# Second-layer weights decoded at other steps, and four places instead of five for the second product, in an attention and two feed-forward layers kernel

## The chip, the cores and the metric

One core of a Trainium2 chip. The metric is the device time of one execution in microseconds. All matrix work runs on TensorE, elementwise work on VectorE and ScalarE; transfers are issued by SyncE (SP) and ScalarE.

## The reference, cut to what matters

```python
def reference(q, k, v, moe_w_in, moe_w_out, moe2_w_in, moe2_w_out):
    # windowed attention: B 4, heads 8, S 576, D 64, window of 64 positions
    scores = q @ k.transpose(0, 1, 3, 2) / sqrt(64)          # masked outside the window
    attn = softmax(scores)
    x = (attn @ v).transpose(0, 2, 1, 3).reshape(2304, 512)
    # first layer, d_ff 2048
    h = x @ moe_w_in
    x = (maximum(h, 0) + log1p(exp(-abs(h)))) @ moe_w_out    # softplus
    # second layer, d_ff 2048
    h = x @ moe2_w_in
    g = where(h >= 1, h, where(h <= -1, 0, (h + 1) ** 2 / 4))
    return g @ moe2_w_out
```

All of it is float32.

## The kernel before

Precision. A float32 product is made of three matmuls of high and low parts (`high`, `low`): high by high, high by low, low by high.

First layer. The 2304 tokens are worked in blocks of 512, 256, 512, 512 and 512 (blocks 0 to 4). A block takes 16 steps, one for each tile f of 128 columns of d_ff (the small block takes two tiles in a step). A step has `g1` (L391, twelve matmuls into a bank h), `softplus` on ScalarE twice (L414 gh, L415 e), the low part on VectorE (L416 gl), and two steps later (LAG) `g2` (L402, twelve matmuls into four banks y). While block i is multiplied, the attention of block i+1 is made in four chunks of 128 tokens, put between the steps as items: score products (L273), copies of the scores (L297 on ScalarE, L301 on VectorE, L295 where a chunk begins a sequence), maximum (L305, L306), eight exponentials (L310) on ScalarE, normalising (L317) into p, transposes of p (L327) on TensorE, masking into pt (L337), products with v (L354), and the two parts of x (L359, L362). Block 4 has no attention beside it. The opening is ordered by a list written by hand (START); after it a scheduler orders each engine's instructions by when they can run.

Weights. w_in and w_out of a tile f lie side by side as 64-bit words, 512 KB of raw words for a half (one of the two matrices' tiles). `load_w` (L145, on SP) brings a half into `raw`, a ring of four buffers shared with o, xs and wf. `begin_half` (L162, ScalarE) and `end_half` (L167, L168, L169, VectorE) turn it into float32 in a bits buffer, of which there are two; these two are also the buffers of c in the second layer. The second layer's 32 halves are decoded in blocks 2 and 3, one at every step of the program (`decode_w`), w_in and w_out in turn (the scheduler brings the first of them forward into block 1), and each is stored to DRAM (wd, L204, 256 KB) at the next step. Later the w_in halves come back in pairs as ab (`load_pair`, L453), and the w_out halves in pairs as wf (`load_wout`, L473), to be split into wh (L178) and wl (L185) in block 4 and in the first two pairs of the second layer.

Second layer. 2304 tokens in three blocks of 768, and in each block eight pairs of tiles f: 24 pairs. x2, the first layer's result, is read back (xs, L493) and cut into pieces (`term` L500, `split_x` L505, L506). A pair is one step of a fast matrix product with seven products (`product`, L535, six matmuls of 384 columns each); `combine` (L459 to L468) makes the seven pieces of w_in. `total` adds (L526) or copies (L524) a bank into c, with m1, u2 and m5 as kept banks; `quadratic` (L513 to L518) is the activation. The second product of the pair before, `second` (L550, six groups of six matmuls of 512 columns), is put between the products by `behind(0)` to `behind(5)`. In the last pair of a block the banks are copied (L553) and stored (L555).

## Time and profile before

| | us |
|---|---|
| three runs | 888.42, 886.96, 892.16 (median 888.42) |
| profiled execution | 889.04 |
| its span, first to last instruction | 887.3 |
| TensorE busy | 848.9 (96%) |
| VectorE busy | 578.4 (65%) |
| ScalarE busy | 409.2 (46%) |

The mean granted clock is 0.998 of full speed. TensorE is named PE in the views, VectorE DVE, ScalarE ACT, SyncE SP. The copies of a finished block into o (L425) begin at 156.4 us for block 0, 217.7 for block 1, 319.8 for block 2, 424.3 for block 3 and 512.9 for block 4; the second layer takes the rest. A name like `a<-ident,p` is what an instruction writes and reads; a name in brackets is what ended the idle time ahead of an instruction.

### The profile page before, as it was taken

Reading aid. Unit: us, or ns where it says so; the run is one execution under the profiler, and the core shown is the slowest. Engines: PE = TensorE matmul, PEld = TensorE weight load, DVE = VectorE, ACT = ScalarE, POOL = GpSimd, SP = SyncE. Lnnn points to the kernel's source line nnn. Section 1 sums busy time; section 2 is a strip of 40 time slices with the busy share of each in tenths; the row PEclk is TensorE's granted clock in tenths of the full one; section 3 lists DMA queues with packets and bytes.
Section 4 is the critical chain, followed back from the end, with each engine's and each line's share of the span. In section 5 each row is a group of like instructions: output and inputs, shape, how many; then the busy total and the mean of one; then the engine's idle time right before and its main releaser. Section 6 shows DMA issues by size and latency. Waiting matters only on the chain.

```text
span 887.3 us, 13141 instructions
## 1 busy us (share of the span) xinstructions
PE 848.9 (96%) x5032; PEld 716.3 (81%) x5032; DVE 578.4 (65%) x1101; ACT 409.2 (46%) x987; POOL 1.5 (0%) x10
## 2 busy tenths in 40 slices
PE   3799999999998999899999999999999999999998
PEld 2686666799877887688888898999898989988896
DVE  5998953764677256635344498667787768776653
ACT  4655622443434344433344474445655446454442
POOL 0000000000000000000000000000000000000000
PEclk9999999999999999999999999999999999999999
DMA  8677512843874157501412041010330101201001
GB/s 299 206 241 233 181 59 80 271 150 119 304 260 155 54 183 249 198 1 48 160 36 89 24 167 48 25 48 24 105 109 24 48 24 47 96 24 49 24 1 71
DMA packets 55118, 100.59 MB, mean 113 GB/s; under 512 B 5904, under 2 KB 25360, under 8 KB 55056
## 3 DMA queue, kind: packets, MB, share of 16 engines
q1 hardware_dynamic: 52672, 95.31, 32.7%
q10 hardware_dynamic: 2384, 4.46, 1.3%
q8 instruction: 39, 0.64, 0.3%
q14 instruction: 23, 0.19, 0.1%
HBM read 81.92 MB, written 17.83 MB: 112 GB/s over the span
## 4 chain that ended last, share of the span: by engine, by line
PE 76%; DMA 10%; DVE 8%; ACT 3%; issue 2%; SPq 1%; ACTq 0%; DVEq 0%
PE h L535 20%; PE y L402 15%; PE y L550 15%; PE h L391 15%; PE a L550 7%; DMA raw<-in_w 6%; DMA wd<-bits 3%; DVE pt L337 2%; DVE bits L168 2%; PE a L354 2%; ACT p L310 1%; DVE bits L169 1%; ACT bits L162 1%; PE a L273 1%; DVE bits L167 1%
## 5 line engine op out<-in xcount | busy, mean ns | idle before, releaser
L391 PE MATMUL h<-xh,area 128*128 128x512 f32 (+1 forms) x672 | 202.6, 371 | 1.7 <-ACT g L409 1.7
L535 PE MATMUL h<-area,ah 128*128 128x384 f32 x672 | 171.3, 335 | 0.0
L391 PEld LDWEIGHTS h<-xh,area 128*128 128x128 f32 x672 | 122.1, 190 | 24.5 <-issue 2.7
L535 PEld LDWEIGHTS h<-area,ah 128*128 128x128 f32 x672 | 123.3, 188 | 10.3
L391 PE MATMUL h<-xl,area 128*128 128x512 f32 (+1 forms) x336 | 121.7, 362 | 0.0
L535 PE MATMUL h<-area,al 128*128 128x384 f32 x336 | 112.5, 335 | 0.0
L514 ACT ACTIVATE e<-e 128x384 f32<-128x384 f32 x96 | 50.2, 524 | 95.9 <-DVE e L513 95.7
L402 PE MATMUL y<-gl,wh 128*128 128x512 f32 (+1 forms) x256 | 93.1, 363 | 0.0
L402 PE MATMUL y<-gh,wh 128*128 128x512 f32 (+1 forms) x256 | 92.9, 363 | 0.0
L402 PE MATMUL y<-gh,wl 128*128 128x512 f32 (+1 forms) x256 | 92.8, 363 | 0.0
L416 DVE TENSOR_TENSOR gl<-e,gh 128x512 fp32r<-128x512 f32 x56 | 38.6, 689 | 65.6 <-ACT e L415 65.6
L550 PE MATMUL y<-wh,gl 128*128 128x512 f32 x192 | 76.2, 397 | 0.0
L550 PE MATMUL y<-wl,gh 128*128 128x512 f32 x192 | 75.8, 395 | 0.0
L550 PE MATMUL y<-wh,gh 128*128 128x512 f32 x192 | 74.6, 389 | 0.0
L391 PEld LDWEIGHTS h<-xl,area 128*128 128x128 f32 x336 | 64.0, 191 | 9.4 <-issue 0.7
L414 ACT ACTIVATE gh<-h 128x512 fp32r<-128x512 f32 x56 | 33.2, 593 | 81.2 <-PE h L391 81.2
L518 DVE TENSOR_TENSOR gl<-e,gh 128x384 fp32r<-128x384 f32 x96 | 53.3, 555 | 18.1 <-ACT gh L517 17.9
L535 PEld LDWEIGHTS h<-area,al 128*128 128x128 f32 x336 | 63.0, 188 | 0.0
L517 ACT CAST gh<-e 128x384 fp32r<-128x384 f32 x96 | 49.3, 514 | 28.8 <-DVE e L515 28.7
L515 DVE TENSOR_TENSOR e<-c,e 128x384 f32<-128x384 f32 x96 | 53.2, 555 | 13.7 <-ACT e L514 12.3
L162 ACT ACTIVATE bits<-raw 128x512 f32<-128x512 f32 x48 | 32.0, 670 | 64.7 <-DMA wd<-bits 30.9
L310 ACT ACTIVATE p<-p,mx 128x64 f32<-128x64 f32 x144 | 48.1, 338 | 23.5 <-DVE mx L306 23.3
(104 smaller groups left out, 1347.5 us busy)
## 6 DMA issues: line engine op xcount, KB each, us to landing
raw<-in_w SPq DMA_DIRECT2D x64, 512.0 KB, 5.3
ab<-wd SPq DMA_DIRECT2D x24, 512.0 KB, 3.3
qt<-in_q SPq DMA_DIRECT2D x34, 256.0 KB, 4.7
vt<-in_v SPq DMA_DIRECT2D x32, 256.0 KB, 3.2
wd<-bits SPq DMA_DIRECT2D x32, 256.0 KB, 3.4
kt<-in_k SPq DMA_DIRECT2D x29, 256.0 KB, 4.7
xs<-x2d SPq DMA_DIRECT2D x12, 384.0 KB, 4.0
wf<-wd SPq DMA_DIRECT2D x8, 512.0 KB, 4.6
```

The costliest lines, as they stand in the source:

```text
L162: A.activation(t.bitcast(F32), raws[j][:, :, 1].bitcast(F32), AF.Copy, scale=2.0 ** -112)
L310: A.activation(k["sel"][:, i, :], k["sel"][:, i, :], AF.Softplus, bias=k["mx"][:, i:i + 1], scale=SCALE, accum_out=k["sm"][:, i:i + 1])
L391: T.matmul(h, w, x, start=i == 0, stop=i == len(ops) - 1)
L402: T.matmul(y[m][:, c0:c0 + n], w, x, start=begin and i == 0, stop=f == NF - 1 and i == len(ops) - 1)
L414: A.activation(gh, h, AF.Softplus)
L416: V.tensor_tensor(gl, e, gh.bitcast(F32), op=ALU.subtract)
L514: A.activation(e, e, AF.Square, bias=0.5, scale=0.5)
L515: V.tensor_tensor(e, c, e, op=ALU.max)
L517: A.copy(gh, e)
L518: V.tensor_tensor(gl, e, gh.bitcast(F32), op=ALU.subtract)
L535: T.matmul(bank, l[:, c], r[:, kc], start=begin and kc == i == 0, stop=kc == 1 and i == 2, skip_group_check=True)
L550: T.matmul(yw[t], l, r, start=p == j == i == 0, stop=p == NQ - 1 and j == 1 and i == 2)
```

## The change

1. Blocks 2 and 3 decode only w_in halves, one at every second step (`decode_win`), and store 16 halves to DRAM instead of 32. `load_w` for the second layer is issued after the store and not after the decode.
2. The w_out halves are decoded where they are split (`split_wout`): one at each step of block 4 from the fifth on (twelve), and one in each of the first four pairs of the second layer. They don't go through DRAM; wf and its eight loads of 512 KB are gone. The number of raw loads stays at 64.
3. x2's first block is read at block 4's first step into buffers of its own (tag g, used later for the activations), and cut at steps 3, 5, ... 15 instead of 9 to 15; the first `combine` comes at step 3 instead of 11.
4. m1 and m5 become one tile m.
5. `behind(1)` moves ahead of the product with S2, so that the second product stands in four places of a pair: two groups, then one, one, two.
6. The last output tile is copied and stored in two halves, VectorE with SP and ScalarE with its own queue.

In the rows below p_ and a number is the tile p of one chunk of attention; numbers and line numbers differ between the two kernels (L310 is now L319, L414 L423, L415 L424, L297 L306, L359 L368).

ScalarE, attention of block 3 in block 2, the chunk whose transposes start at 271.60 in the trace; before:

```order
L359 CAST xh<-a 128x4x128
L162 ACTIVATE bits<-raw 128x512
L414 ACTIVATE gh<-h 128x512
L415 ACTIVATE e<-h 128x512
L162 ACTIVATE bits<-raw 128x512
L297 COPY p_2582<-a 128x256 x2
L162 ACTIVATE bits<-raw 128x512
L310 ACTIVATE p_2582,sm<-p_2582,mx 128x64
L414 ACTIVATE gh<-h 128x512
L415 ACTIVATE e<-h 128x512
L310 ACTIVATE p_2582,sm<-p_2582,mx 128x64 x7
```

and now:

```order
L368 CAST xh<-a 128x4x128
L423 ACTIVATE gh<-h 128x512
L424 ACTIVATE e<-h 128x512
L306 COPY p_2540<-a 128x256 x2
L319 ACTIVATE p_2540,sm<-p_2540,mx 128x64 x2
L423 ACTIVATE gh<-h 128x512
L424 ACTIVATE e<-h 128x512
L319 ACTIVATE p_2540,sm<-p_2540,mx 128x64 x6
```

Four decoding steps stood among the cast ahead, the copies and the exponentials, and none does now; the exponentials are parted after the second and not after the first.

ScalarE, the first chunk that is made in block 3 (transposes at 348.16); before:

```order
L415 ACTIVATE e<-h 128x512
L162 ACTIVATE bits<-raw 128x512 x2
L297 COPY p_3305<-a 128x256 x2
L414 ACTIVATE gh<-h 128x512
L415 ACTIVATE e<-h 128x512
L310 ACTIVATE p_3305,sm<-p_3305,mx 128x64 x8
```

and now:

```order
L424 ACTIVATE e<-h 128x512
L162 ACTIVATE bits<-raw 128x512 x2
L306 COPY p_3215<-a 128x256 x2
L319 ACTIVATE p_3215,sm<-p_3215,mx 128x64
L423 ACTIVATE gh<-h 128x512
L424 ACTIVATE e<-h 128x512
L319 ACTIVATE p_3215,sm<-p_3215,mx 128x64 x7
```

The two decoding steps ahead of the copies stay; the softplus pair moved from ahead of the exponentials to behind the first of them.

ScalarE, from the first decoding step of block 2 to its first chunk's copies; before:

```order
L162 ACTIVATE bits<-raw 128x512
L414 ACTIVATE gh<-h 128x512
L415 ACTIVATE e<-h 128x512
L162 ACTIVATE bits<-raw 128x512
L359 CAST xh<-a 128x4x128
L414 ACTIVATE gh<-h 128x512
L415 ACTIVATE e<-h 128x512
L162 ACTIVATE bits<-raw 128x512 x2
L297 COPY p_2346<-a 128x256 x2
```

and now:

```order
L162 ACTIVATE bits<-raw 128x512
L423 ACTIVATE gh<-h 128x512
L424 ACTIVATE e<-h 128x512
L162 ACTIVATE bits<-raw 128x512
L368 CAST xh<-a 128x4x128
L162 ACTIVATE bits<-raw 128x512
L423 ACTIVATE gh<-h 128x512
L424 ACTIVATE e<-h 128x512
L162 ACTIVATE bits<-raw 128x512 x2
L306 COPY p_2320<-a 128x256 x2
```

Four decoding steps were ahead of the copies, and five are now.

```diff
@@ -141,9 +141,9 @@
             j = wnext[0]
             if j < (2 if wlimit[0] else 4) * NF:
                 raw = spool.tile([P, DM, 2], I32, tag="raw", name="raw", bufs=NRAW)
-                src = (w1, w2)[j // (2 * NF)][j // 2 % NF]
-                e.dma_start(
-                    raw.rearrange("p c w -> p (c w)"), src[:, 2 * DM * (j % 2):2 * DM * (j % 2 + 1)])
+                f, part = divmod(j, 2) if j < 2 * NF else (j % NF, j // NF - 2)
+                e.dma_start(raw.rearrange("p c w -> p (c w)"),
+                            (w1, w2)[j // (2 * NF)][f, :, 2 * DM * part:2 * DM * (part + 1)])
                 raws[j] = raw
                 wnext[0] += 1
 
@@ -167,7 +167,7 @@
         V.tensor_scalar(t, t, 3, 1, op0=ALU.logical_shift_left, op1=ALU.bitwise_or)
         V.scalar_tensor_tensor(t, hi, -2 ** 31, t, op0=ALU.bitwise_and, op1=ALU.bitwise_or)
         V.scalar_tensor_tensor(t, lo, 29, t, op0=ALU.logical_shift_right, op1=ALU.bitwise_or)
-        if not opening[0]:
+        if not opening[0] and j < 2 * NF:
             load_w()
 
     def high(key, t, part):
@@ -199,15 +199,24 @@
     def keep_w():
 
         while kept:
-            j = kept.pop()
-            f, part = divmod(j - 2 * NF, 2)
-            nc.sync.dma_start(wd[part][f // 2][:, DM * (f % 2):DM * (f % 2 + 1)], decoded.pop(j).bitcast(F32))
-
-    def decode_w(j):
+            f = kept.pop()
+            nc.sync.dma_start(wd[f // 2][:, DM * (f % 2):DM * (f % 2 + 1)], decoded.pop(2 * NF + f).bitcast(F32))
+            load_w()
+
+    def decode_win(f):
         keep_w()
+        begin_half(2 * NF + f)
+        end_half(2 * NF + f)
+        kept.append(f)
+
+    def split_wout(f):
+        j = 3 * NF + f
         begin_half(j)
         end_half(j)
-        kept.append(j)
+        t = decoded.pop(j).bitcast(F32)
+        high((1, f), t, 1)
+        low((1, f), t, 1)
+        load_w()
 
 
 
@@ -433,10 +442,10 @@
 
 
     PIECES = ("A11", "A12", "A22", "S1", "S2", "S3", "S4")
-    TERMS = ("B11", "B21", "T2", "T1", "T3", "B22", "T4")
     halves = {}
     wins = {}
-    slots = {t: i for i, t in enumerate(TERMS)}
+    FIRST = ("B11", "T1", "B22", "T3", "T2", "B21", "T4")
+    slots = {t: i for i, t in enumerate(FIRST)}
     spare = [7, 8, 9]
     l1 = {}
 
@@ -444,13 +453,13 @@
 
         apool_guard.__exit__(None, None, None)
         l1["pool"] = ctx.enter_context(tc.tile_pool(name="second", bufs=1))
-        for m in ("m1", "u2", "m5"):
+        for m in ("m", "u2"):
             l1[m] = l1["pool"].tile([P, NW], F32, name=m)
 
     def load_pair(k):
 
         halves[k] = l1["pool"].tile([P, 4, 256], F32, tag="ab", name="ab")
-        nc.sync.dma_start(halves[k].rearrange("p a c -> p (a c)"), wd[0][k % NQ])
+        nc.sync.dma_start(halves[k].rearrange("p a c -> p (a c)"), wd[k % NQ])
 
     def combine(k):
         a = halves.pop(k)
@@ -468,17 +477,6 @@
         V.tensor_tensor(lo[:, 2], a[:, 3], hi[:, 2].bitcast(F32), op=ALU.subtract)
         wins[k] = (hi, lo)
 
-    def load_wout(p):
-        t = spool.tile([P, 2 * DM], F32, tag="raw", name="wf", bufs=NRAW)
-        nc.sync.dma_start(t, wd[1][p])
-        return t
-
-    def split_wout(p, t):
-        for i in range(2):
-            src = t[:, DM * i:DM * (i + 1)]
-            high((1, 2 * p + i), src, 1)
-            low((1, 2 * p + i), src, 1)
-
     def piece(slot):
         at = 1536 * slot
         return [cut(at + o, 768).rearrange("p (a t) -> p a t", a=2) for o in (0, 768)]
@@ -488,7 +486,10 @@
     def load_x2(blk):
 
         for name, kc, hf in (("B11", 0, 0), ("B12", 0, 1), ("B22", 2, 1), ("B21", 2, 0)):
-            st = spool.tile([P, 2, NW], F32, tag="raw", name="xs", bufs=NRAW)
+            if blk:
+                st = spool.tile([P, 2, NW], F32, tag="raw", name="xs", bufs=NRAW)
+            else:
+                st = l1["pool"].tile([P, 2, NW], F32, tag="g", name="xs", bufs=4)
             t0 = WIDE * blk + NW * hf
             nc.sync.dma_start(st, x2d[kc:kc + 2, :, t0:t0 + NW].rearrange("m p t -> p m t"))
             xt[name] = st
@@ -550,9 +551,14 @@
                 T.matmul(yw[t], l, r, start=p == j == i == 0, stop=p == NQ - 1 and j == 1 and i == 2)
         if p == NQ - 1:
             o = spool.tile([P, DM], F32, tag="raw", name="o", bufs=NRAW)
-            (A.copy if t % 2 else V.tensor_copy)(o, yw.pop(t))
-            r = WIDE * blk + t * P
-            (nc.scalar if t % 2 else nc.sync).dma_start(out[r:r + P, :], o)
+            r = slice(WIDE * blk + t * P, WIDE * blk + (t + 1) * P)
+            if WIDE * (blk + 1) == NT and t == ORDER[-1]:
+                for copy, e, c in ((V.tensor_copy, nc.sync, slice(0, DM // 2)), (A.copy, nc.scalar, slice(DM // 2, DM))):
+                    copy(o[:, c], yw[t][:, c])
+                    e.dma_start(out[r, c], o[:, c])
+            else:
+                (A.copy if t % 2 else V.tensor_copy)(o, yw.pop(t))
+                (nc.scalar if t % 2 else nc.sync).dma_start(out[r, :], o)
 
 
     def emit(item, i, g):
@@ -658,30 +663,25 @@
             if f + kf == NF:
                 wlimit[0] = False
                 load_w(3)
-        if 2 <= i <= 3:
-            decode_w(2 * NF + NF * (i - 2) + f)
+        if 2 <= i <= 3 and f % 2:
+            decode_win(NF // 2 * (i - 2) + f // 2)
 
         if i == last:
             if f == 0:
                 keep_w()
                 begin_second()
-            if f % 2 == 0:
-                p = f // 2 - 2
-                if p >= 0:
-                    split_wout(p, fetched.pop(p))
-                if p + 1 >= 0 and f + 2 < NF:
-                    fetched[p + 1] = load_wout(p + 1)
-            if f == 8:
                 load_x2(0)
                 load_pair(0)
-            for step, name in enumerate(("B11", "T1", "B22", "T3", "T2", "B21", "T4")):
-                if f == 9 + step:
-                    if name[0] == "T":
-                        term(name)
-                    split_x(name, slots[name])
-            if f == 11:
+            if f == 3:
                 combine(0)
                 load_pair(1)
+            if f >= 4:
+                split_wout(f - 4)
+            if f % 2 and f > 1:
+                name = FIRST[f // 2 - 1]
+                if name[0] == "T":
+                    term(name)
+                split_x(name, slots[name])
         h = pt("h")[:, :kf * n]
         for j in range(kf):
             g1(f + j, c0, n, *xs[i], h[:, j * n:(j + 1) * n])
@@ -689,9 +689,10 @@
             emit_g2(pend.pop(0))
         pend.append((i, f, kf, c0, n, softplus(h, kf * n, i > 0)))
     gfree = [[gpool.tile([P, 512], F32R, tag=t, name=t)[:, :NW] for t in ("gh", "gl")] for _ in range(3)]
-    gfree += [[l1["pool"].tile([P, NW], F32R, tag=t, name=t, bufs=3) for t in ("gh", "gl")] for _ in range(3)]
+    wide = [l1["pool"].tile([P, 2, NW], F32R, tag="g", name="g", bufs=4) for _ in range(3)]
+    gfree += [[t[:, 0], t[:, 1]] for t in wide]
     gold = {}
-    m1, u2, m5 = [l1[m] for m in ("m1", "u2", "m5")]
+    m, u2 = l1["m"], l1["u2"]
     rest = [lambda it=it, ms=ms: emit_g2(it, ms) for it in pend for ms in (range(2), range(2, 4))]
     rest = [rest[0], rest[1], None, rest[2], rest[3], None]
 
@@ -707,8 +708,8 @@
                 combine(k + 1)
             if k + 2 < NQ * NT // WIDE:
                 load_pair(k + 2)
-            if blk == 0 and p < 2:
-                split_wout(p + 6, load_wout(p + 6))
+            if blk == 0 and p < 4:
+                split_wout(p + 12)
             turn = blk + 1 < NT // WIDE
             if turn and p == NQ - 4:
                 load_x2(blk + 1)
@@ -731,23 +732,23 @@
             g = {}
             a, b = [pt("h")[:, :NW] for _ in range(2)]
             product(a, "A11", "B11", w, True)
-            A.copy(m1, a)
+            A.copy(m, a)
             product(b, "A12", "B21", w, True)
 
             x, y = gfree.pop(), gfree.pop()
-            g[0, 0] = total(b, m1, x)
+            g[0, 0] = total(b, m, x)
             behind(0)
             renew("T2", "B11")
+            behind(1)
+            renew("T1", "B21")
             product(a, "S2", "T2", w, False)
             A.copy(u2, a)
-            behind(1)
-            renew("T1", "B21")
             product(b, "S1", "T1", w, True)
-            A.copy(m5, b)
+            A.copy(m, b)
             behind(2)
             renew("T3", "T2")
             product(a, "S3", "T3", w, False)
-            g[1, 1] = total(a, m5, y)
+            g[1, 1] = total(a, m, y)
             product(b, "S4", "B22", w, False)
             g[0, 1] = total(b, u2, gold[0, 1] if gold else gfree.pop())
             behind(3)
```

## Rows read from the trace of the kernel before

**Rows 1.** Waits of TensorE in the whole span: total us, times, longest.
```profile
PE a L327 <- DVE p L317: 9.6, 5, 3.0
...
PE a L354 <- DVE pt L337: 2.3, 5, 0.8
```

**Rows 2.** Windows: length, then busy us (instructions) of each engine, PEclk, DMA share, GB/s.
```profile
154.00:200.00 46.00, 43.42 (x453) 38.80 (x451) 30.34 (x60) 21.98 (x76) 0.00 (x0) 1.00 0.64 207
200.00:260.00 60.00, 59.19 (x463) 49.67 (x462) 38.24 (x68) 25.01 (x69) 0.00 (x0) 1.00 0.66 215
260.00:300.00 40.00, 37.73 (x224) 30.54 (x223) 25.12 (x48) 16.90 (x55) 0.00 (x0) 1.00 0.47 159
300.00:360.00 60.00, 58.55 (x394) 47.15 (x393) 33.00 (x59) 24.55 (x69) 0.00 (x0) 1.00 0.60 195
360.00:396.00 36.00, 32.98 (x220) 26.35 (x219) 16.96 (x33) 13.12 (x43) 0.00 (x0) 0.95 0.24 79
396.00:506.00 110.00, 110.00 (x518) 91.29 (x517) 46.80 (x71) 42.43 (x81) 0.00 (x0) 1.00 0.21 70
```

**Rows 3.** Timeline of TensorE: start, us, instruction, [idle before <-releaser].
```profile
271.60 0.63 PE L327 MATMUL a<-ident,p 128*128 128x128 f32 x4 [2.05 <-DVE p L317]
...
348.16 0.63 PE L327 MATMUL a<-ident,p 128*128 128x128 f32 x4 [1.45 <-DVE p L317]
...
351.37 0.39 PE L402 MATMUL y<-gh,wh 128*128 128x512 f32 x1
...
376.20 1.08 PE L327 MATMUL a<-ident,p 128*128 128x128 f32 x4 [3.02 <-DVE p L317]
...
380.95 0.39 PE L402 MATMUL y<-gh,wh 128*128 128x512 f32 x1
```

**Rows 4.** Timeline of ScalarE at two decoding steps and behind them.
```profile
261.99 0.66 ACT L162 ACTIVATE bits<-raw 128x512 f32<-128x512 f32 x1 [4.75 <-DMA wd<-bits]
...
365.37 1.31 ACT L162 ACTIVATE bits<-raw 128x512 f32<-128x512 f32 x2 [4.33 <-DMA wd<-bits]
366.58 0.64 ACT L297 COPY p<-a 128x256 f32<-128x256 f32 x2
```

**Rows 5.** Timeline of TensorE, the score products ahead of the wait at 376.20.
```profile
360.93 1.10 PE L273 MATMUL a<-kt,qt 64*64 64x128 f32 x32
```

**Rows 6.** DMA issues of the page: count, KB each, us to landing.
```profile
raw<-in_w SPq DMA_DIRECT2D x64, 512.0 KB, 5.3
...
wd<-bits SPq DMA_DIRECT2D x32, 256.0 KB, 3.4
```

**Rows 7.** Groups of instructions in 160 to 400 us: busy us, mean ns, idle before.
```profile
L168 DVE SCALAR_TENSOR_TENSOR bits<-raw,bits 128x512 int32<-128x512 int32 x32 | 22.0, 691 | 0.9
...
L162 ACT ACTIVATE bits<-raw 128x512 f32<-128x512 f32 x32 | 21.3, 669 | 53.7 <-DMA wd<-bits 30.9 <-DMA raw<-in_w 9.8 <-issue 5.6
...
L167 DVE TENSOR_SCALAR bits<-bits 128x512 int32<-128x512 int32 x32 | 13.5, 424 | 23.4 <-ACT bits L162 23.2
```

**Rows 8.** Windows of two pairs of the second layer, columns as in rows 2.
```profile
528.10:543.80 15.70, 15.70 (x80) 14.13 (x79) 15.04 (x31) 8.05 (x18) 0.00 (x0) 1.00 0.11 33
543.80:559.40 15.60, 15.60 (x80) 14.04 (x79) 10.60 (x23) 7.35 (x16) 0.00 (x0) 1.00 0.11 35
```

**Rows 9.** Timeline of TensorE in one pair, the first matmul of each group.
```profile
590.57 0.39 PE L550 MATMUL a<-wh,gh 128*128 128x512 f32 x1
...
593.33 0.51 PE L535 MATMUL h<-area,ah 128*128 128x384 f32 x2
...
595.44 0.39 PE L550 MATMUL y<-wh,gh 128*128 128x512 f32 x1
...
596.83 0.51 PE L535 MATMUL h<-area,ah 128*128 128x384 f32 x2
...
597.87 0.39 PE L550 MATMUL y<-wh,gh 128*128 128x512 f32 x1
```

**Rows 10.** Timeline of VectorE, the last instruction.
```profile
883.21 0.69 DVE L553 COPY o<-a 128x512 f32<-128x512 f32 x1 [2.03 <-PE a L550]
```

More of the change, by code (lines that the diff above doesn't have):

```diff
@@ L114, in tile_window_attention_two_ffn @@
     x2d = dpool.tile([KC, P, NT], F32, name="x2d")
-    wd = [[dpool.tile([P, 2 * DM], F32, name=f"wd{part}{p}") for p in range(NQ)] for part in range(2)]
+    wd = [dpool.tile([P, 2 * DM], F32, name=f"wd{p}") for p in range(NQ)]
     area = hold.tile([P, 2 * NF * DM], F32R, name="area")
@@ L635, in tile_window_attention_two_ffn @@
     start()
-    fetched = {}
     for i, f, kf, c0, n in steps:
```

## The prediction

> **What bounds the kernel now.** I read the waits of TensorE first, then the windows by stage, then the timeline of each engine around the waits that are left. The list of waits [rows 1] shows what the matmul engine still loses after the opening: transposes of the attention that wait for the normalised probabilities p (9.6 us in five waits) and products with v that wait for the masked copies pt (2.3 us in five). The windows [rows 2] say where. TensorE is short of its window by 2.58 us in 154 to 200, 0.81 in 200 to 260, 2.27 in 260 to 300, 1.45 in 300 to 360 and 3.02 in 360 to 396, all inside blocks 1 to 3; in the 110 us from 396 to 506 (the end of block 3 and most of block 4) it misses nothing. So no work taken off another engine can help there: what can be won lies in the waits of blocks 2 and 3.
>
> The single waits [rows 3]: 2.05 us before the transposes at 271.60, 1.45 before those at 348.16, 3.02 before those at 376.20. The last one costs more than itself. After it the four transposes take 1.08 us instead of 0.63, and from their start to the first L402 matmul pass 380.95 - 376.20 = 4.75 us, against 351.37 - 348.16 = 3.21 for the same work after the 1.45 wait. That is 1.54 us at the lower of the two clock levels; the granted clock of this stretch is 0.95 [rows 2].
>
> Who makes p late? ScalarE runs its instructions in the order they stand. At 261.99 a decoding step (L162) has waited 4.75 us, at 365.37 another one 4.33 us, both for the store of a decoded half to DRAM, which holds one of the two bits buffers [rows 4]. The score copies (L297) stand behind them. At the second place the scores are ready at 360.93 + 1.10 = 362.03 [rows 5], and the copies start at 366.58 [rows 4], 4.55 us late; maximum, exponentials and normalising follow, and p comes 3.02 us too late.
>
> **The change, part by part.** Decoding at every second step. Blocks 2 and 3 decode 16 halves instead of 32, 16 of the 32 stores of 256 KB go (3.4 us each from issue to landing [rows 6]), and each removed half takes 0.67 us from ScalarE and 0.42 + 2 x 0.69 = 1.80 from VectorE (L167, L168 and the like L169) [rows 7]. What counts is where the rest ends up. The order shows no decoding step between the cast ahead of the chunk of 271.60 and its copies any more (its first place), nor ahead of that of 376.20; their exponentials follow the copies as in chunks that never wait. I take both as gone: the 2.27 of the window 260 to 300, 3.02, the 1.54 of clock behind it, and about 0.7 of the 0.81 in 200 to 260, a pt wait inside a burst that gets shorter. Sum 7.53. If pt's wait and the smaller one in 260 to 300 stayed, 6.6.
>
> What stays: the 2.58 of 154 to 200 comes from the raw loads of the first burst, which the change keeps. Block 3's first chunk (348.16) keeps two decoding steps ahead of its copies, and its exponentials are now broken by a softplus pair that stood before them. Two ScalarE instructions of 128x512 bound that by 2 x 0.67 = 1.34 [rows 7], so the wait is 1.45 to 2.79; from below I let it fall to 0.8, since one store less runs beside it. I take the middle of the upper pair, 2.1: a loss of 0.65, with no clock step, because after 2.05 us at 271.60 the transposes took the short 0.63 [rows 3].
>
> The w_out halves, decoded where they are used. Twelve now fall into block 4, four into the first four pairs. The loads of stored pairs (wf) and their second pass through DRAM go, which the list of TensorE's waits never shows as a cause: nothing. The splits (wh, wl) were there before; new in a step of block 4 are 0.67 us of ScalarE and 1.80 of VectorE. Twelve times that is 8.0 and 21.6 us, on top of 42.43 and 46.80 in 110 us [rows 2]: 46% and 62% busy. Nothing on the path, as long as the softplus of a step is not held behind a decode; between nothing and the slow rival below. The raw loads take 5.3 us in the median [rows 6], four are in flight, one step needs one.
>
> Splits of the first x2 earlier, into buffers of their own, and the first combine at step 3: the same instructions in an idle-free stretch, nothing.
>
> Four decodes in pairs 0 to 3: VectorE had 15.04 us in the 15.70 of the fullest pair and TensorE was still busy all through [rows 8]; the next pair had 10.60. With 1.80 more the light pairs have room; where splits of the next x2 fall together with a decode, VectorE is at its limit. I take +0.3, between 0 and 2.3 (below).
>
> The order in a pair. Two groups of six L550 matmuls go together. Twelve in a row take 593.33 - 590.57 = 2.76, six take 596.83 - 595.44 = 1.39 [rows 9], so a pair gains 0.02, all 24 pairs 0.5 at most and nothing at least; I take 0.2. The price: the copy of u2 now has 1.39 + 1.04 = 2.43 us until S3 overwrites its bank, not 3.82 (1.39 for six L550, 1.04 for six L535 [rows 9]). Two other copies of the pair already live with the same 2.43 and show no wait: nothing. Sharing m between two sums only lets a copy wait for an addition that ended several groups before.
>
> The last output tile in two halves. The last copy takes 0.69 us [rows 10] with TensorE finished; half the columns on each of two engines save 0 to 0.35, and I take 0.3 with a little from the smaller transfer. On that transfer the Trainium skill speaks against more: its page DMA: Bandwidth & Descriptors, section Issuing engines are not separate DMA queues, says that transfers started by different engines run on the same 16 DMA engines and only the issue time is saved. By it the two halves together land no sooner than the one tile and only the copy's half counts; no row of the kernel before has a split tile.
>
> **Sum.** -7.53 + 0.65 + 0.3 - 0.2 - 0.3 = -7.1 us. Against the profiled execution of 889.04 us (887.3 of span and 1.7 around it) that is 881.9; against the median of the three runs, 888.42, which is 0.6 lower, 881.3. I put 881.6.
>
> **Rivals.** (a) The waits move instead of going. The bursts are still set by when ring buffers come free, and the order puts five decoding steps, one more than before, ahead of the copies of block 2's first chunk. If block 3's first wait grows to the 3.02 of 376.20 and takes the clock step, that is 3.02 + 1.54 - 2.1 = 2.5 more than forecast; one more decode (0.67) ahead of block 2's first chunk plus its VectorE part gives 1.2. 881.6 + 3.7 = 885.3. For it: both wait patterns exist in the trace. Against: fewer stores compete for the two bits buffers. 0.20.
>
> (b) VectorE becomes the bound for a while in the first pairs. 15.04 + 1.80 = 16.84 in a pair of 15.7 [rows 7, 8], 1.15 too much, in two pairs 2.3: 883.9. Against: durations overlap a little at their ends, and only some pairs are full. 0.10.
>
> (c) The wait of about 2 us at block 3's first chunk takes the clock down as the 3.02 one did, since it may come nearer to 2.79 than to 2.05: 881.6 + 1.54 = 883.1. Against: after 2.05 us the transposes took 0.63, not 1.08 [rows 3]. The Trainium skill, page TensorE: Matmul & The Clock Gate, section HAM oscillation, says that idle gaps between bursts of matmuls throw the clock back to half; by that rule, taken for every gap, this rival would be the forecast. The trace agrees with it for the longest of the three waits only. 0.06.
>
> (d) Slower: block 4's chain. On ScalarE wh now waits for the three VectorE steps of its half, and the next decode and the next step's softplus stand behind it; if this loop takes longer than a step, every one of twelve steps is late. With 1 us each: 12 - 7.1 = 4.9 more than before, 893.3 from the median's 888.4 (893.9 from the profiled one); it decides from about 0.96 us a step. For it: the same kind of queueing makes the waits of today. Against: the two engines are at 46% and 62% by the sum above, and each raw half is loaded steps ahead. 0.06.
>
> (e) It doesn't do what it says: the copies wait for something else as soon as the stores are gone (raw loads, of which the number stays at 64), and all waits come back in place: 888.4. Against: the releasers named at 261.99 and 365.37 are both stores. 0.06.
>
> **How the numbers follow.** The forecast has 0.52. A difference of 0.5%, 4.4 us, is about what a measurement of this kernel can tell from no change, so faster means under 884.0 and slower over 892.9. Faster: the forecast, (c) and most of (b), 0.52 + 0.06 + 0.08 = 0.66. Within 0.5%: (a), (e) and the rest of (b), 0.20 + 0.06 + 0.02 = 0.28. Slower: (d), 0.06. For the range the good ends are: block 3's wait down to 0.8 (1.3 better), the whole 0.5 of the pairs, no new wait in them (0.3), which with the spread of 0.6 between the two sums gives 878.8 or so; the bad end takes in (b), (a) at 885.3 and somewhat above. 878.6 to 887.0 leaves out (d), (e) and little else.
>
> **What would show it.** Right: no wait of L327 for p near the places of 271.60 and 376.20, a granted clock of 1.00 from 360 to 396, one wait of about 2 us at block 3's first chunk, TensorE idle-free through block 4 and the pairs, pairs of 15.6 us, 16 stores to wd and no wf. Wrong: waits of L402 for wl, wh or gl in block 4, of L535 for the bank or for al in pairs 1 to 4, a wait of over 2.5 us with long transposes behind it at block 3's first chunk, or a new one at block 2's first.

## The result, and the profile after

The changed kernel takes 879.72 us (median of four, 879.26 to 880.32) against 888.62 of the kernel before in the same comparison: ratio 0.9895, 95% interval 0.9864 to 0.9926, so 8.9 us faster where 7.1 were forecast. Its profiled execution took 879.26 us with a span of 877.5; the one of before had 889.04 and 887.3, so the two traces differ by 9.8. Of the executions further below, one of e9 (1214.52 us at a mean granted clock of 0.665) ran in a slow state and is left out.

The waits of TensorE that answer to [rows 1] (line 326 is the old 317, 336 the old 327, 346 and 363 the old 337 and 354):

```profile
PE a L336 <- DVE p L326: 2.7, 3, 2.1
...
PE a L363 <- DVE pt L346: 1.7, 2, 0.9
```

Five waits for p of 9.6 us in all have become three of 2.7, and 2.1 of these are one wait. The windows that answer to [rows 2]:

```profile
154.00:200.00 46.00, 43.73 (x454) 39.19 (x455) 27.30 (x53) 20.67 (x74) 0.00 (x0) 1.00 0.55 173
200.00:260.00 60.00, 60.00 (x468) 50.41 (x467) 36.51 (x69) 24.89 (x71) 0.00 (x0) 1.00 0.56 180
260.00:300.00 40.00, 40.00 (x256) 32.56 (x256) 14.12 (x25) 13.75 (x49) 0.00 (x0) 1.00 0.17 54
300.00:360.00 60.00, 59.81 (x410) 48.09 (x407) 33.64 (x61) 24.56 (x71) 0.00 (x0) 1.00 0.55 180
360.00:396.00 36.00, 36.00 (x216) 29.34 (x215) 13.64 (x25) 12.69 (x45) 0.00 (x0) 1.00 0.06 17
396.00:506.00 110.00, 110.00 (x523) 92.17 (x522) 67.49 (x111) 51.47 (x89) 0.00 (x0) 1.00 0.30 103
```

TensorE is short by 2.27 us in the first window (2.58 before), by 0.19 in 300 to 360 (1.45), and by nothing in 200 to 260 (0.81), 260 to 300 (2.27) and 360 to 396 (3.02); the granted clock of the last is 1.00 and not 0.95. In 396 to 506 VectorE's work has risen from 46.80 to 67.49 and ScalarE's from 42.43 to 51.47, and TensorE is still full; the window that holds the same work as that of before begins 9.6 us sooner (386.4 to 496.4) and has 64.75 and 49.16. Of the stores, 16 are left, and their landing is no shorter ([rows 6]: 3.4):

```profile
wd<-bits SPq DMA_DIRECT2D x16, 256.0 KB, 4.1
```

The transposes that answer to [rows 3], the first product of the second layer and the last matmul, on TensorE's timeline:

```profile
169.15 0.63 PE L336 MATMUL a<-ident,p 128*128 128x128 f32 x4 [2.12 <-DVE p L326]
...
268.47 0.60 PE L336 MATMUL a<-ident,p 128*128 128x128 f32 x4
...
343.31 0.63 PE L336 MATMUL a<-ident,p 128*128 128x128 f32 x4 [0.19 <-DVE p L326]
...
368.17 0.60 PE L336 MATMUL a<-ident,p 128*128 128x128 f32 x4
...
492.75 0.51 PE L536 MATMUL h<-area,ah 128*128 128x384 f32 x2
...
873.57 0.39 PE L551 MATMUL a<-wh,g 128*128 128x512 f32 x1
```

Three rows of the kernel before for the same places:

```profile
168.74 0.63 PE L327 MATMUL a<-ident,p 128*128 128x128 f32 x4 [2.18 <-DVE p L317]
...
502.32 0.51 PE L535 MATMUL h<-area,ah 128*128 128x384 f32 x2
...
882.79 0.39 PE L550 MATMUL a<-wh,gl 128*128 128x512 f32 x1
```

Place by place the difference grows like this: at block 1's wait the changed kernel is 168.74 - 169.15 = 0.4 us behind (its opening was that much longer in this execution); at the chunk of 271.60 it is 3.1 ahead, at 348.16 4.9, at 376.20 8.0, at the first product of the second layer 502.32 - 492.75 = 9.6, at the last matmul 9.2, at the end of the span 9.8. So nearly everything is won between 185 and 385 us, nothing in block 4, 0.4 is lost in the second layer, and 0.6 is won behind the last matmul, most of it because that end was slow in the trace of before (see e8).

The one place where I had forecast a loss was block 3's first chunk: 1.45 us of waiting before, 2.1 expected, 0.19 found. Before, on SP, VectorE, ScalarE and TensorE:

```profile
321.56 9.09 SPq L145 DMA_DIRECT2D raw<-in_w  x4
...
332.34 0.42 SPq L204 DMA_DIRECT2D wd<-bits  x1
332.85 0.38 SPq L145 DMA_DIRECT2D raw<-in_w  x1
333.29 0.48 SPq L204 DMA_DIRECT2D wd<-bits  x1
```

```profile
329.18 0.69 DVE L169 SCALAR_TENSOR_TENSOR bits<-raw,bits 128x512 int32<-128x512 int32 x1
```

```profile
338.12 0.66 ACT L162 ACTIVATE bits<-raw 128x512 f32<-128x512 f32 x1 [5.18 <-issue]
...
340.62 0.64 ACT L297 COPY p<-a 128x256 f32<-128x256 f32 x2
...
344.08 0.35 ACT L310 ACTIVATE p<-p,mx 128x64 f32<-128x64 f32 x1 [1.84 <-DVE mx L306]
```

```profile
334.45 1.10 PE L273 MATMUL a<-kt,qt 64*64 64x128 f32 x32
```

And after:

```profile
317.98 8.35 SPq L145 DMA_DIRECT2D raw<-in_w  x4
...
328.11 1.06 SPq L203 DMA_DIRECT2D wd<-bits  x2
329.27 1.41 SPq L145 DMA_DIRECT2D raw<-in_w  x2
```

```profile
325.09 0.69 DVE L169 SCALAR_TENSOR_TENSOR bits<-raw,bits 128x512 int32<-128x512 int32 x1
```

```profile
332.44 1.28 ACT L162 ACTIVATE bits<-raw 128x512 f32<-128x512 f32 x2 [3.09 <-DMA wd<-bits]
...
333.63 0.63 ACT L306 COPY p<-a 128x256 f32<-128x256 f32 x2
...
338.26 0.35 ACT L319 ACTIVATE p<-p,mx 128x64 f32<-128x64 f32 x1 [4.00 <-DVE mx L315]
```

```profile
330.87 1.10 PE L282 MATMUL a<-kt,qt 64*64 64x128 f32 x32
```

In both kernels SP has four raw loads to issue (9.09 us before, 8.35 after; it waits in between for the stores of finished tiles o, which share the ring), then two loads of v, and comes to the first store about as long behind the last VectorE step of that half: 332.34 behind 329.18 + 0.69 = 329.87 before, 328.11 behind 325.09 + 0.69 = 325.78 after, so 2.5 and 2.3 us. What differs comes next. Before, a raw load goes out between the first store and the second; after, the two stores leave together and the raw loads follow. The first decoding step that needs a buffer runs 5.8 us behind its store before (338.12) and 4.3 us after (332.44); before, the profile names no releaser for it, and that it is the buffer is inferred. The second one follows before at 340.05, behind a wait of 1.27 us, and after at once. So the copies come 5.07 us after the scores were ready before (334.45 + 1.10) and 1.66 us after them now (330.87 + 1.10): 3.41 us sooner.

Behind the copies it goes the other way. The first exponential starts 344.08 - 340.62 = 3.46 us behind them before and 338.26 - 333.63 = 4.63 now, and the eight exponentials take 3.64 us and not 2.67, since the softplus pair stands among them. That gives 2.14 us back, and what is left, 1.27, is the fall of the wait from 1.45 to 0.19.

The Trainium skill, page DMA: Bandwidth & Descriptors, section Queues, rings and completion order, says that a ring's descriptors are consumed in order, so that a store starts behind the loads issued ahead of it; the trace agrees as far as it goes, in that the store behind four raw loads held its buffer for 5.8 and 4.3 us, more than the median landing of 3.4 [rows 6] and 4.1. The load of the next raw half now stands behind the store in the program; it is in the first point of the section on the change, and the prediction gives it no price.

### The profile page after: what moved, and what is told of

Its sections match the earlier page's. It is cut to its first block, busy times and chain, and to the rows that moved or that the text cites. A ratio compares the mean times of both kernels' runs of the same rounds, so it can differ in the third digit from the quotient of the medians.

```text
span 877.5 us, 13083 instructions
## 1 busy us (share of the span) xinstructions
PE 846.5 (96%) x5032; PEld 715.5 (82%) x5032; DVE 578.1 (66%) x1101; ACT 411.6 (47%) x988; POOL 1.5 (0%) x10
## 4 chain that ended last, share of the span: by engine, by line
PE 88%; DMA 5%; DVE 4%; ACT 2%; issue 1%; SPq 1%; ACTq 0%
PE h L400 20%; PE y L411 20%; PE h L536 20%; PE y L551 15%; PE a L551 8%; DMA raw<-in_w 3%; PE a L363 2%; PE a L282 1%; DMA first<-in_q 1%; PE a L336 1%; ACT p L319 1%; DVE pt L346 1%; DMA wd<-bits 0%; DVE bits L168 0%; ACT bits L162 0%
## 5 line engine op out<-in xcount | busy, mean ns | idle before, releaser
L536 PE MATMUL h<-area,ah 128*128 128x384 f32 x672 | 171.5, 336 | 0.0
L536 PEld LDWEIGHTS h<-area,ah 128*128 128x128 f32 x672 | 123.2, 188 | 8.1 <-DVE c L527 0.2
L536 PE MATMUL h<-area,al 128*128 128x384 f32 x336 | 112.9, 336 | 0.0
L551 PE MATMUL y<-wh,g 128*128 128x512 f32 x244 | 88.5, 393 | 0.0
L423 ACT ACTIVATE gh<-h 128x512 fp32r<-128x512 f32 x56 | 33.3, 595 | 68.9 <-PE h L400 68.8
L536 PEld LDWEIGHTS h<-area,al 128*128 128x128 f32 x336 | 63.0, 188 | 0.0
L319 ACT ACTIVATE p<-p,mx 128x64 f32<-128x64 f32 x144 | 48.1, 339 | 22.8 <-DVE mx L315 22.8
L411 PE MATMUL y<-g,wo 128*128 128x512 f32 (+1 forms) x160 | 57.5, 507 | 0.0
L527 DVE TENSOR_TENSOR c<-h,m 128x384 f32<-128x384 f32 x48 | 26.6, 554 | 46.9 <-PE h L536 46.2
L411 PEld LDWEIGHTS y<-gl,wh 128*128 128x128 f32 x256 | 48.3, 189 | 7.6
L411 PEld LDWEIGHTS y<-gh,wh 128*128 128x128 f32 x256 | 48.3, 189 | 7.5
L411 PEld LDWEIGHTS y<-gh,wl 128*128 128x128 f32 x256 | 48.3, 189 | 7.5
```

Source lines behind the costliest of these rows:

```text
L319: A.activation(k["sel"][:, i, :], k["sel"][:, i, :], AF.Softplus, bias=k["mx"][:, i:i + 1], scale=SCALE, accum_out=k["sm"][:, i:i + 1])
L411: T.matmul(y[m][:, c0:c0 + n], w, x, start=begin and i == 0, stop=f == NF - 1 and i == len(ops) - 1)
L423: A.activation(gh, h, AF.Softplus)
L527: V.tensor_tensor(c, bank, other, op=ALU.add)
L536: T.matmul(bank, l[:, c], r[:, kc], start=begin and kc == i == 0, stop=kc == 1 and i == 2, skip_group_check=True)
L551: T.matmul(yw[t], l, r, start=p == j == i == 0, stop=p == NQ - 1 and j == 1 and i == 2)
```

## Experiments

The theory of the prediction (A): a decoding step ahead of the score copies makes p late, so fewer decoded halves take the waits away. The rival that the result suggests (B): what held the copies up was a bits buffer whose store left late, behind raw loads in SP's queue, and the order of load and store does the work. Times are medians beside runs of the kernel before on the same chip (889.23 us for e1 to e4, 889.69 for e5 to e8, 888.45 for e9, e11 and e12).

**e1: the load ahead of the store again.** In the changed kernel:

```diff
-        if not opening[0] and j < 2 * NF:
+        if not opening[0] and j < 3 * NF:
             load_w()
...
             nc.sync.dma_start(wd[f // 2][:, DM * (f % 2):DM * (f % 2 + 1)], decoded.pop(2 * NF + f).bitcast(F32))
-            load_w()
```

> The changed kernel, with only the order of load and store undone: in blocks 2 and 3 the next raw load is issued right after a half is decoded again, ahead of that half's store. Theory A (what stands ahead of the score copies on ScalarE decides, and the number of decoded halves sets that): no change, 879.7 +- 0.5, and the wait at block 3's first chunk stays at about 0.2 us. Theory B (the store that frees a bits buffer stood behind raw loads in SP's queue; the store-first order is what took block 3's first wait away): that wait comes back to 1.5 to 2.8 us, 881.0 to 882.5.

883.85 us (ratio 0.9953, interval 0.993 to 0.9976): more than B said. Its profiled execution was the slowest of seven, 887.6. TensorE there:

```profile
168.29 1.09 PE L335 MATMUL a<-ident,p 128*128 128x128 f32 x4 [2.09 <-DVE p L325]
...
253.00 0.76 PE L362 MATMUL a<-pt,vt 128*64 128x64 f32 x16 [2.20 <-issue]
...
351.63 0.63 PE L335 MATMUL a<-ident,p 128*128 128x128 f32 x4 [1.51 <-DVE p L325]
```

The wait at block 3's first chunk is back (1.51), there is a new one of 2.20 in block 2, for which the profile names no releaser and whose cause stays open, and one of 0.65 at 185.37. But the places of 271.60 and 376.20 have no wait: fewer halves are enough there without the moved load. So the whole change without the order of load and store gives 5.4 us; beside e3 and e4, which keep the order and ran in the same comparison (879.09 and 879.53), it lacks 4.3 to 4.8.

**e2: the store first, and nothing else.** In the kernel before:

```diff
-        if not opening[0]:
+        if not opening[0] and j < 2 * NF:
             load_w()
...
             nc.sync.dma_start(wd[part][f // 2][:, DM * (f % 2):DM * (f % 2 + 1)], decoded.pop(j).bitcast(F32))
+            load_w()
```

> The kernel before, with the raw load moved behind the store and nothing else: 32 halves are still decoded in blocks 2 and 3. Theory A: the waits before the transposes of block 3's chunk in block 2 (2.05 us) and of block 3's second chunk (3.02 us, with 1.54 of clock) stay within a microsecond, 886 to 889. Theory B: the stores land earlier, and these waits shrink to under 1 us each, 881 to 883.

882.88 us (0.993, 0.991 to 0.9949), the time that B gave. The transposes of the three chunks, in order:

```profile
270.81 0.60 PE L328 MATMUL a<-ident,p 128*128 128x128 f32 x4
...
346.89 0.63 PE L328 MATMUL a<-ident,p 128*128 128x128 f32 x4 [1.43 <-DVE p L318]
...
371.76 0.62 PE L328 MATMUL a<-ident,p 128*128 128x128 f32 x4
```

With all 32 halves decoded the waits of 2.05 and 3.02 us are gone, and the one at block 3's first chunk stays, although the store goes first there too. The third chunk, TensorE and ScalarE in e2, and the first exponential in the kernel before:

```profile
359.67 1.10 PE L274 MATMUL a<-kt,qt 64*64 64x128 f32 x32
```

```profile
364.48 0.63 ACT L298 COPY p<-a 128x256 f32<-128x256 f32 x2
...
367.68 0.35 ACT L311 ACTIVATE p<-p,mx 128x64 f32<-128x64 f32 x1 [1.57 <-DVE mx L307]
```

```profile
371.16 0.35 ACT L310 ACTIVATE p<-p,mx 128x64 f32<-128x64 f32 x1 [3.95 <-DVE mx L306]
```

The same two decoding steps stand ahead of the copies as in [rows 4]. Three things are shorter. The copies start 3.71 us after the scores (359.67 + 1.10) instead of 4.55. The first exponential starts 367.68 - 364.48 = 3.20 us behind them and not 371.16 - 366.58 = 4.58: the first of the two halves was decoded 1.25 us after the scores (362.02) and not 3.34 (365.37), so less of VectorE's decoding work stands ahead of the maximum. And the softplus pair (L415, L416) now runs between the copies and the first exponential, while the maximum is still being made; in the kernel before it stood behind the first exponential and held the other seven up, so the eight take 2.66 us instead of 3.63. Together that is 3.2 us: 0.8 in the copies, 1.4 in the maximum, 1.0 in the exponentials. The last is not the buffer's doing: moving a DMA in the program also moved the softplus pair, since the scheduler orders each engine anew. How much of the rest is the buffer and how much the new order, the edit can't part. SP issues the store of that buffer at once in both kernels (360.04 before, 357.91 in e2, each 0.03 us behind VectorE's last step), and the buffer is in use again 5.3 and 4.1 us later; so it is the landing that got shorter, and not the time until SP comes to the store.

**e5: half of the stores left out.** In the kernel before, the load ahead of the store as there; it leaves the stores of the w_out halves out, so its output is not the reference's:

```diff
-            nc.sync.dma_start(wd[part][f // 2][...], decoded.pop(j).bitcast(F32))
+            t = decoded.pop(j)
+            if not part:
+                nc.sync.dma_start(wd[part][f // 2][...], t.bitcast(F32))
...
-        nc.sync.dma_start(t, wd[1][p])
+        nc.sync.dma_start(t, wd[0][p])
```

> The kernel before, with all 32 halves decoded and the raw load ahead of the store as there, but the 16 w_out halves not stored; the later loads of stored w_out read the stored w_in halves, so the result is not the reference's. Theory B in the form 'a store that lands late holds one of the two bits buffers': with half the stores the score copies of block 3's chunk in block 2 and of block 3's second chunk start earlier and their waits (2.05, 3.02) go, 881 to 884. Rival (the decoding work on ScalarE and VectorE itself is what delays the copies): both waits stay over 1 us, 886 to 889.

881.9 us (0.9921, 0.9896 to 0.9945). The chunk of 271.60 has no wait, and block 3's first one has 1.93:

```profile
267.71 0.60 PE L329 MATMUL a<-ident,p 128*128 128x128 f32 x4
...
344.28 0.63 PE L329 MATMUL a<-ident,p 128*128 128x128 f32 x4 [1.93 <-DVE p L319]
```

All the decoding work is still there, and the two long waits are gone, so the work alone doesn't make them. But the theory that the copies start earlier holds at one place only: at 376.20 they come 0.05 us after the scores, at 271.60 they come 4.01 us after them, as late as before (4.14). Here too the scheduler set the instructions anew.

**e4: every step of block 2.** In the changed kernel:

```diff
-        if 2 <= i <= 3 and f % 2:
-            decode_win(NF // 2 * (i - 2) + f // 2)
+        if i == 2:
+            decode_win(f)
```

> The changed kernel, with its 16 w_in halves decoded at every step of block 2 instead of every second step of blocks 2 and 3. Theory A in the form 'how dense': the waits of block 2 come back (0.7 and 2.3 us), block 3 has none: 882.0 to 883.0. In the form 'how many': 16 halves are 16, no wait over 0.5 us returns: 879.3 to 880.0.

879.53 us (0.9887, 0.9872 to 0.9902): as the changed kernel. Its trace has no wait for p or pt behind one of 0.61 us at 183.81. How dense the steps stand in the program made no difference to the time.

**The three parts of a chunk.** From ScalarE's and TensorE's timelines, us: for the chunk whose transposes stand at that place in the kernel before, how long after the end of the scores the copies start, how long after that the first exponential starts, how long the eight exponentials take, and TensorE's wait.

| place | kernel | copies | first exponential | exponentials | wait |
|---|---|---|---|---|---|
| 271.60 | before | 4.14 | 4.01 | 3.63 | 2.05 |
| | changed, e1 | 0.06 | 2.20 | 3.74 | none |
| | e2 | 3.58 | 2.87 | 2.67 | none |
| | e4 | 4.16 | 2.85 | 2.66 | none |
| | e5 | 4.01 | 2.84 | 2.68 | none |
| 348.16 | before | 5.07 | 3.46 | 2.67 | 1.45 |
| | changed | 1.66 | 4.63 | 3.64 | 0.19 |
| | e1 | 5.13 | 3.45 | 2.67 | 1.51 |
| | e2 | 2.85 | 4.69 | 3.64 | 1.43 |
| 376.20 | before | 4.55 | 4.58 | 3.63 | 3.02 |
| | changed, e1 | 0.05 | 2.20 | 3.75 | none |
| | e2 | 3.71 | 3.20 | 2.66 | none |

The sum of the three parts tells the wait. Where it is under 9.7 us there is none, and where it is more the wait is the sum less 9.74, to 0.02 us (11.78 before at 271.60, 12.76 at 376.20). So copies that come 4.16 us late cost nothing in e4, where nothing else is long, and in the kernel before 4.14 us cost 2.05, since a decoding step and a softplus pair stood behind them. With fewer halves (changed, e1) the copies come at once at two places; at block 3's first chunk only fewer halves and the moved load together shorten the sum below 10.

**e3: five places again.** In the changed kernel:

```diff
-            behind(1)
-            renew("T1", "B21")
             product(a, "S2", "T2", w, False)
             A.copy(u2, a)
+            behind(1)
+            renew("T1", "B21")
```

> The changed kernel, with the second product back in five places of a pair (the group behind(1) after the copy of u2 again). If joining two groups of six saves 0.02 us a pair as the prediction took: 0.5 us slower at most, 880.0 to 880.2, and a pair of 15.66 against 15.64. Rival (the joining saves nothing, a pair is 15.64 both ways): 879.5 to 879.8; the 0.36 us lost in pairs 1 and 2 may go or stay.

879.09 us (0.9886, 0.987 to 0.9903). The changed kernel on TensorE, by the first L536 matmul of the third, fourth and fifth pair:

```profile
521.24 0.51 PE L536 MATMUL h<-area,ah 128*128 128x384 f32 x2
...
537.13 0.51 PE L536 MATMUL h<-area,ah 128*128 128x384 f32 x2
...
552.84 0.51 PE L536 MATMUL h<-area,ah 128*128 128x384 f32 x2
```

And e3, the first and the third pair:

```profile
491.62 0.51 PE L536 MATMUL h<-area,ah 128*128 128x384 f32 x2
...
520.40 0.51 PE L536 MATMUL h<-area,ah 128*128 128x384 f32 x2
```

In the changed kernel the first two pairs last 521.24 - 492.75 = 28.49 us, the third 537.13 - 521.24 = 15.89, the fourth 15.71, the fifth 15.64; before, the first two lasted 28.45 and each of the next ones 15.64. With five places the first two last 520.40 - 491.62 = 28.78, the third 15.64 and the fourth 15.69. So five places lose as much as four, 0.3 to 0.4 us, only earlier, and the traces of e6, e7, e8 and e11 (five places) and of e1, e4 and e12 (four) repeat it. Joining two groups gives nothing that shows and costs nothing. In the changed kernel's third pair a decode and a split of x2 fall together: the third L551 matmul of a group starts 0.38 us after the second (523.58, 523.96) and not 0.23, behind VectorE's step L519 that makes the low part of the activation (523.35 to 523.90).

**e6, e8: the last tile.** e6 is e3 with an output tile for each half, e8 is e3 with one copy and one store of the whole tile. The edit of e6:

```diff
+                    o = spool.tile([P, DM // 2], F32, tag="raw", name="o", bufs=NRAW)
-                    copy(o[:, c], yw[t][:, c])
-                    e.dma_start(out[r, c], o[:, c])
+                    copy(o, yw[t][:, c])
+                    e.dma_start(out[r, c], o)
```

> The changed kernel with the second product in five places (as e3), and the two halves of the last output in a tile of their own each. In the changed kernel's profile ScalarE's half waits 1.23 us and starts when VectorE's half is done (874.46 after 874.00 + 0.43). If the shared tile is what orders them, both copies start together and the end comes 0.4 us earlier: 878.6 to 878.8 against e3's 879.1, and 0.4 less between TensorE's last matmul and the end of the span. If the bank of PSUM that both read orders them, nothing changes.

> e3 with the last output tile copied and stored as one, as in the kernel before. The prediction took 0.3 us for the split; the two profiles show 4.54 us from the last matmul's start to the end of the span before and 3.96 after. If the split is the cause: 0.5 to 0.6 more than e3, 879.6 to 879.7, and 4.5 us at the end. If half as large a transfer saves nothing and only the copy counts: 0.2 to 0.3.

880.13 us (0.9902, 0.9879 to 0.9925) and 880.12 (0.9899, 0.9875 to 0.9922): equal, and within each other's spread. In the changed kernel the two halves don't run side by side, and with two tiles in e6 they don't either:

```profile
874.00 0.43 DVE L557 COPY o<-a 128x256 f32<-128x256 f32 x1 [2.03 <-PE a L551]
```

```profile
874.46 0.37 ACT L557 COPY o<-a 128x256 f32<-128x256 f32 x1 [1.23 <-DVE o L557]
```

ScalarE's half begins 0.46 us behind VectorE's, when that is done (1.23 us of waiting, 874.00 + 0.43); in e6 it is 875.46 behind 875.00, the same. With separate output tiles, what the two copies still share is the bank they read; that this orders them is inferred. The Trainium skill, page PSUM — Partial Sum Buffer, section PSUM bank collisions raise a hardware error, says that two engines must not touch the same quarter of the partitions of one bank at once, reads against reads included, and that the compiler makes one wait for the other; the trace agrees. From the start of the last matmul to the end of the span pass 887.3 - 882.79 = 4.5 us before, 877.5 - 873.57 = 3.9 after, and 877.3 - 873.18 = 4.1 in e8. The trace of before is the odd one: e2, e5 and e9, which also store the tile whole, have 4.1 like e8, and the seven other traces with the split have 3.9 to 4.0. So the split is worth 0.1 to 0.2 us, and the median can't tell it.

**e7: raw loads let go earlier.** e6 with

```diff
-            if f + kf == NF:
+            if f == 0:
                 wlimit[0] = False
                 load_w(3)
```

> e6, and the first three raw loads of the second layer's weights let go at block 1's first step instead of its last. The order then has no decoding step between the score copies and the exponentials of the chunk whose transposes wait 2.1 us at 169 us. If that step's wait for its raw half (3.3 us) is the cause, the wait goes: 2.0 us less than e6, 876.6 to 877.0. Rival: the earlier loads and stores collide with the last loads of the first layer's weights, and a wait of about the same size appears before 160 us: 878.5 or more.

876.68 us (0.9863, 0.9836 to 0.989), 3.5 under e6 in the same comparison. In the changed kernel a decoding step stands ahead of the first exponential of the chunk at 169 us and waits for its raw half; in e7 the exponentials follow the copies with only the maximum between them:

```profile
164.50 0.68 ACT L162 ACTIVATE bits<-raw 128x512 f32<-128x512 f32 x1 [3.31 <-DMA raw<-in_w]
```

```profile
161.97 0.35 ACT L319 ACTIVATE p<-p,mx 128x64 f32<-128x64 f32 x1 [1.56 <-DVE mx L315]
```

There is no wait at 169 us any more. The first three halves are decoded in block 0 (their stores leave by 119.3 us), where no new wait appears. At block 3's first chunk 0.66 us are left.

**e9, e11, e12: one chip.** e9 is e2 with the edit of e7, e11 is e7 again, e12 the changed kernel again.

> The kernel before with two moves of loads and nothing else: the raw load behind the store (as e2), and the first three raw loads of the second layer's weights at block 1's first step (as e7). All 32 halves are still decoded in blocks 2 and 3 and stored. Theory B (order of loads and stores alone gives most of the gain): the waits at 169 us (2.2) and those of 2.05 and 3.02 us are gone, only that at block 3's first chunk (1.4) is left, 880 to 881, and the rest to the version of e7 (876.7) is that wait, the split of the last tile and what fewer halves save besides. Theory A (fewer halves are needed): waits of over 1 us stay in block 2 or at block 3's second chunk, 883 or more.

> The kernel of e7 again, beside the changed kernel on the same chip. As measured before: 876.2 to 877.7, so 2.5 to 3.5 us under the changed kernel. If the difference came from the chip: within 1 us of it.

> The changed kernel itself, on the same chip as the two others. As measured before: 879.3 to 880.3; the wait at 169 us about 2.1, at block 3's first chunk 0.2, and 0.3 lost in the first two pairs.

880.75 us for e9 (0.9922, 0.9892 to 0.9951), 877.47 for e11 (0.9881, 0.9855 to 0.9908), 881.48 for e12 (0.9924, 0.9896 to 0.9951), whose runs spread more than before, from 878.92 to 883.32. So two moves of loads in the kernel before do as much as the whole change, and e11, with both moves and fewer halves, is 4.0 us under the changed kernel here. The changed kernel gained 7.0 us in this comparison and 8.9 in the first. What e9 still waits for:

```profile
168.33 0.63 PE L328 MATMUL a<-ident,p 128*128 128x128 f32 x4 [1.47 <-DVE p L318]
...
343.94 0.63 PE L328 MATMUL a<-ident,p 128*128 128x128 f32 x4 [1.74 <-DVE p L318]
...
369.74 0.63 PE L328 MATMUL a<-ident,p 128*128 128x128 f32 x4 [0.79 <-DVE p L318]
```

B had only block 3's first wait left, so its time came true and two of its waits didn't go. At 168.33 another decoding step stands ahead of the exponentials now and waits 2.65 us for its raw half (163.67). Together the three are 4.0 us, against 0.15 in e11's trace after 110 us: that is about what fewer halves are worth beside the order of the loads, and it covers the 3.3 us between the two medians.

## Why the prediction was right

The time lies in the range and the gain is 8.9 us for 7.1. Point by point:

- The waits at 271.60 and 376.20, the clock step behind the second and the pt wait at 251 were taken as gone, 7.53 us. They are: 268.47 and 368.17 stand without a wait, the clock is 1.00. The reason given holds: with fewer halves the copies come 0.05 us after the scores at both places, in e1 too, where the load is not moved. It is not the only way: the moved load alone (e2) takes both waits away with copies 3.6 to 3.7 us late. So the gains don't add: 5.4 us without the moved load, 6.4 with it alone, 8.9 and 7.0 for the change in two comparisons.
- The prediction's "who makes p late" stopped at the copies. They are one part of three; the decoding work ahead of the maximum and the softplus pair among the exponentials are the others, and only the sum over 9.7 us is waited for.
- The step that failed is "a loss of 0.65" at block 3's first chunk; 1.26 us were won instead. The bound from above took the softplus pair alone, 1.34; behind the copies 2.14 us were lost (0.97 in the exponentials, 1.17 in the maximum). What it had no price for is that the copies come 3.41 us sooner. SP comes to the store no sooner than before (2.3 us behind the half for 2.5). Neither the moved load alone (e2, 1.43) nor fewer halves alone (e1, 1.51) takes the wait away; both together do. This term alone, 1.9 us, is about the whole difference between 7.1 and 8.9; the smaller misses cancel, and the 7.0 of the second comparison shows that the gain isn't known that closely.
- What stays: the wait at 169 us was to stay and did, 2.12 for 2.18. e7 shows its cause, a decoding step ahead of the exponentials that waits for its raw load.
- Block 4: nothing, as forecast. The two engines have 64.75 and 49.16 us of 110 in the window with the same work, where 68.4 and 50.4 were worked out, and TensorE has no gap. Rival (d) had no place to start.
- The first pairs: +0.3 taken, 0.32 found (15.89 and 15.71 against 15.64). This is rival (b) at a seventh of its price; five places in e3 lose as much.
- Joining groups: 0.2 taken, nothing found. A difference of 0.02 us, worked out from rows that show two digits, was no ground for it.
- The last tile: 0.3 taken, 0.1 to 0.2 found. What the smaller transfer saves couldn't be told apart, since the copies ran one after the other.
- Rival (a), waits that move, didn't come in the changed kernel, but in e1 one did: 2.20 us in block 2, where nothing was expected. Rival (e) didn't come either: no wait of over 0.2 us is left in place behind 169 us.

## What to carry to other kernels

When a long chain ends in a wait, measure each of its parts in the kernel with the wait and in one without, before naming one: here copies 4 us late cost 2 us or nothing, depending on what stood behind them. Price every moved DMA of a change, the ones that only change places too: a load that could wait, moved behind a store, was worth 6.4 us here, with no work taken away. By what path is shown in part only, since the scheduler then orders the engines anew; so read its new order for the instructions around the wait. An early decoding step whose load lands late holds up all that stands behind it on ScalarE, so let its load go a stage sooner (3.5 us between e6 and e7; in e9, with all 32 halves, the next decoding step took its place and 1.5 us of waiting stayed).

## What was not expected of the hardware

Waits of about the same length did and didn't take the clock down. Behind 2.05 and 2.18 us in the kernel before and 2.12 in the changed one the next transposes ran at the higher level (0.63 us for four, granted clock 1.00); so it was behind 2.28 when the changed kernel was run again (e12). Behind 2.09 us in e1 the same four took 1.09, behind 2.19 in e2 0.73, and the granted clock from 168 to 176 us was 0.79 in both; behind 3.02 in the kernel before they took 1.08. A wait's length alone didn't tell which it would be. And in the profiled execution of the changed kernel the granted clock was 0.52 from 20 to 40 us, in the opening, where TensorE is busy for 11.48 of the 20 us; block 1's wait came only 0.4 us later than in the kernel before, where it was 1.00, and the execution was the fastest of its four. The window of that stretch:

```profile
20.00:40.00 20.00, 11.48 (x126) 9.53 (x120) 18.33 (x35) 10.58 (x42) 0.00 (x0) 0.52 0.64 219
```
